# Attention block and MLP on one core: turned tiles loaded behind their stores, six residual tiles put into their PSUM bank, differences in another order, w2 jobs moved

## The chip, the cores and the metric

The kernel runs on one core of one Trainium2 chip. The metric is the device time of one execution in microseconds (us); lower is better. TensorE multiplies matrices, VectorE (DVE), ScalarE (ACT) and GpSimd (POOL) work on tiles of 128 partitions, and SyncE (SP) and GpSimd issue most DMA transfers. Each engine runs its instructions in the order in which they stand in the program; a wait on one holds up all behind it on that engine.

## The reference: what is computed

One transformer block on `x` (2048 tokens of 512 floats), all in float32, with a linear attention of 32 heads of 16 and an MLP of width 1792. Six rows of 512 (shifts, scales and gates) come from the condition `c`.

```python
mod = (silu(c) @ w_mod).reshape(1, 6, 1, -1)
sa, ca, ga, sb, cb, gb = (mod[:, i] for i in range(6))
h = layernorm(x) * (1 + ca) + sa
q, k, v = heads(h @ wqkv)
pq, pk = phi(q), phi(k)                 # t + 1 where t > 0, else exp(t); plus 1e-6
o = (pq @ (pk^T v)) / (pq . sum(pk) + 1e-6)
x = x + ga * (o @ wo)
h = layernorm(x) * (1 + cb) + sb
x = x + gb * (mish(h @ w1 + b1) @ w2)
```

## The kernel before, in words

**Numbers.** A float32 product is made of three: each operand is split into an upper part `..h` (ACT, L82) and a lower part `..l`, the rest (DVE, L88), and upper x upper, upper x lower and lower x upper are added up in one PSUM bank (`mm3`, L72). One such matmul of 128x512 is a row of 0.23 us on TensorE.

**Blocks and units.** The tokens are four blocks `b` of 512, each four tiles `t` of 128. A bank is a tile of tag `acc` (four buffers), `h` (three) or `tp` (one). After the attention's sums, these units follow on TensorE, named by what they write:

- `q_unit(b, g)` (L330): the queries of a block, 12 matmuls.
- `attend(b)` (L878): the denominators `den`; DVE makes `rden` of them, a DMA stores it (`rden_d`, L890), four DMAs read it back, each row for 16 partitions (`rd`, L894), and DVE multiplies the queries by it (L902), before they are split into `qs_g h` and `qs_g l` for the four groups `g`. For blocks 0 and 1 POOL issues these DMAs, for 2 and 3 SP.
- `o_unit(b, t)` (L921), here unit n = 4b + t: 12 matmuls of `qs` with the output matrix `m`. `o_post` (L912) adds the residual tile `r` (that is `x`) to the bank on DVE (L914).
- For blocks 0 and 1 `norm_first` (L928) follows: the sums of the row and of its squares on ACT (`act_sums`, L213; for tiles 2 and 3 of block 1 bn_stats on DVE), the power -1/2 on POOL (L199), the normalised tile `n` on ACT (L208), and `turn` (L235), a transpose of 32x32 squares on DVE into a buffer `wide` (L239), of which there is one. After a block's last tile `spread` (L241) stores `wide` in DRAM in four DMAs (L245), and `load_squares` (L249) loads the turned block in four (L252). `WAIT` says how many steps the loads stand behind the stores: three for block 0, one for block 1.
- `turned_f` (L983): ACT scales the loaded tile into `hf_n` (L256). The first MLP product works on blocks 0 and 1 at once, as a 2x2 block product in seven multiplications; `columns` (L990) makes the differences `t1` to `t4` of the four `hf_n` of a column half c on DVE (L995), and all are split: b11, b21, b22, t1 to t4.
- `pair_begin` (L1146) multiplies a11 with b11 for a pair g of MLP columns, and ACT copies it to a second bank `p11` (L1149). `pair_early`, `pair_middle` and `pair_end` (L1166 to L1190) make the other products, the next ones with b21, t2, t1 and t3. `d_unit` (L1111) is the second MLP product of one column tile `f`.
- `w2_job(f)` (L707) multiplies tile f of `w2` with the gate `gb` on DVE (L716), splits it and has POOL store both parts (L728); `w2_sums(g)` (L739) makes the differences of tiles 2g and 2g + 1 for the last two blocks, which are done with seven products too.

**What sets the order.** The program is written out by hand. Work beside TensorE is a generator that is started by `spawn`; every `tick()` runs each for one more step, so a `yield` puts the rest one tick later. `order` (L1074) says at which unit n the turned tiles are scaled on ACT: block 0 at n = 9 and 11, block 1 at 12 and 13. `load_w2(0)` and `(1)` come at n = 4, `(2)` and `(3)` at n = 7, where `w2_job(0)` and `w2_job(1)` start too. Two `pair_begin` follow n = 13, then n = 14 and 15, then the pairs.

## Time and profile before

| | us |
|---|---|
| median of 3 runs | 495.13 |
| lowest and highest | 493.16, 496.28 |
| the profiled execution, its own time | 495.35 |
| its span, first to last instruction | 493.6 |

TensorE is busy for 477.6 us of the span (97%), DVE for 396.8 (80%), ACT for 306.2 (62%), POOL for 119.6 (24%). The granted clock of TensorE was 0.993 of full speed in the mean.

How to read the views. A row of the timeline has the start of an instruction in us, its duration, the engine, the line, and out<-in; in brackets stands the idle time before it and what ended that. Instructions on an engine overlap a little, so the distance of two starts is what one costs in a row. Names in the profile leave buffer numbers out: `qs_0h` is the upper part of group 0, whichever block. SPq and POOLq are DMA issues. In the table by stretches the columns are the stretch, busy time of each engine with the count of instructions, the granted clock, the DMA engines' busy share and GB/s.

### The profile page before, as it was taken

The numbers are of one execution on the slowest core, as the hardware profiler recorded it, in microseconds if no ns is written. First come the engines' busy times: TensorE is split into PE (matmuls) and PEld (weight loads), VectorE is DVE, ScalarE is ACT, GpSimd is POOL, SyncE is SP. The second block draws the span as 40 slices with busy tenths as digits, with TensorE's granted clock in tenths as the row PEclk, the third lists the DMA queues.
The fourth block names the chain that finished last, engine by engine and source line by source line (L and its number), as shares of the span: only waits on it lengthen the run. The fifth ranks groups of instructions, "written<-read, shape, count | busy, mean of one in ns | idle before, by whom it ended". The sixth has DMA issues, their size and how long they took to land.

```text
span 493.6 us, 7008 instructions
## 1 busy us (share of the span) xinstructions
PE 477.6 (97%) x2290; PEld 388.7 (79%) x2290; DVE 396.8 (80%) x791; ACT 306.2 (62%) x549; POOL 119.6 (24%) x200
## 2 busy tenths in 40 slices
PE   8999999999999995889999999999999999999997
PEld 6688777768878883678888888888888888888887
DVE  6899897998999895898799874599535678769993
ACT  6787469756656863678777764696055677547600
POOL 3573121000023122113225323233111101263400
PEclk9999999999999998899999999999999999999999
DMA  8905759534874449856468827998472523486974
GB/s 295 378 10 93 185 112 275 190 129 123 255 203 106 139 119 283 265 175 212 160 203 277 233 87 189 390 323 225 122 200 64 107 46 79 113 212 146 233 154 109
DMA packets 86399, 89.10 MB, mean 180 GB/s; under 512 B 22961, under 2 KB 59321, under 8 KB 86362
## 3 DMA queue, kind: packets, MB, share of 16 engines
q1 hardware_dynamic: 61320, 53.37, 37.9%
q0 software_dynamic: 22784, 34.49, 26.1%
q10 hardware_dynamic: 2258, 0.79, 0.8%
q8 instruction: 18, 0.29, 0.2%
q14 instruction: 19, 0.16, 0.1%
HBM read 59.52 MB, written 27.00 MB: 175 GB/s over the span
## 4 chain that ended last, share of the span: by engine, by line
PE 66%; DVE 16%; DMA 9%; ACT 4%; SPq 2%; issue 1%; POOL 1%; DVEq 0%; ACTq 0%
PE p_a L1139 15%; PE p_s L1139 8%; PE oacc L76 5%; PE oacc L75 5%; PE oacc L74 5%; PE m L76 5%; PE m L74 5%; PE m L75 5%; PE p L1139 4%; DMA sq_x<-wide_x 3%; PE pq_a L376 2%; DMA w2r<-in_w_dram 2%; DMA sq_n<-wide_n 2%; DVE wm L175 2%; DVE q L290 1%; DVE q L902 1%
## 5 line engine op out<-in xcount | busy, mean ns | idle before, releaser
L1144 DVE TENSOR_TENSOR cb<-p_s,u 128x512 f32<-128x512 f32 x28 | 19.1, 685 | 11.3 <-ACT u L1179 11.3
L777 POOL DMA_DIRECT2D wb<-w2d x14 | 9.8, 705 | 67.3 <-issue 23.9
L1131 ACT ACTIVATE ub<-cb,b1c 128x512 f32<-128x512 f32 x28 | 20.0, 718 | 6.7 <-DVE cb L1144 6.5
L1149 ACT ACTIVATE p<-p_a 128x512 f32<-128x512 f32 x14 | 8.0, 578 | 24.2 <-PE p_a L1139 12.2
L199 POOL TENSOR_TENSOR rs_n<-rs_n,half 128x1 f32<-128x1 f32 x16 | 9.6, 602 | 52.0 <-DVE rs_n L225 43.3
L1430 POOL DMA_DIRECT2D wt_m<-w2t x20 | 14.0, 703 | 25.2 <-DVE cb L1144 12.4
L256 ACT ACTIVATE hf_n<-sq_n,mc 128x512 f32<-128x512 f32 x16 | 12.3, 807 | 10.8 <-DMA sq_n<-sq_n 10.8
L1179 ACT ACTIVATE u<-p_a 128x512 f32<-128x512 f32 x14 | 8.4, 598 | 17.0 <-PE p_a L1139 16.9
L1106 ACT ACTIVATE u<-p,b1c 128x512 f32<-128x512 f32 x14 | 9.6, 686 | 13.7 <-PE p L1139 13.7
L890 POOL DMA_DIRECT2D rden_d<-rden x2 | 1.5, 738 | 59.9 <-DVE rden L888 59.9
L1106 ACT ACTIVATE u<-p_a,b1c 128x512 f32<-128x512 f32 x14 | 9.6, 688 | 9.2 <-PE p_a L1139 9.1
L783 POOL DMA_DIRECT2D w2b<-w2d x20 | 10.6, 539 | 19.2 <-PE oacc L76 14.1
L74 PE MATMUL o<-m_0h,qs_0h 128*128 128x512 f32 x16 | 6.8, 428 | 6.4 <-ACT qs_0h L82 6.4
L290 DVE SCALAR_TENSOR_TENSOR ku<-e_k,relu_k 128x512 f32<-128x512 f32 x16 | 10.9, 682 | 2.0 <-ACT relu_k L288 2.0
L290 DVE SCALAR_TENSOR_TENSOR q<-e_q,relu_q 128x512 f32<-128x512 f32 x16 | 10.6, 685 | 1.4 <-ACT relu_q L288 1.4
L199 POOL TENSOR_TENSOR rs_x<-rs_x,half 128x1 f32<-128x1 f32 (+1 forms) x10 | 7.8, 787 | 15.9 <-DVE rs_x L194 15.1
L190 DVE BATCH_NORM_STATS2 st_x<-x 128x6 f32<-128x512 f32 x13 | 8.8, 676 | 3.2 <-DMA x<-in_x_dram 3.2
L919 POOL DMA_DIRECT2D x1d<-r x8 | 4.4, 548 | 28.3 <-DVE r L914 28.3
L287 ACT ACTIVATE e_k<-pk 128x512 f32<-128x512 f32 x16 | 9.4, 590 | 2.6 <-PE pk L76 1.7
L914 DVE TENSOR_TENSOR r<-o,r 128x512 f32<-128x512 f32 x16 | 10.8, 675 | 0.0
L175 DVE SCALAR_TENSOR_TENSOR wm<-wm,sc_row 128x512 f32<-128x512 f32 x16 | 10.5, 680 | 0.0
L299 POOL DMA_DIRECT2D ku<-ku x8 | 7.2, 940 | 13.5 <-DVE ku L290 13.5
(1661 smaller groups left out, 1880.9 us busy)
## 6 DMA issues: line engine op xcount, KB each, us to landing
wm<-in_wmodt_dram SPq DMA_DIRECT2D x24, 256.0 KB
w1p<-in_w_dram SPq DMA_DIRECT2D x24, 256.0 KB
w2b<-w2d POOLq DMA_DIRECT2D x20, 256.0 KB, 6.8
wt_m<-w2t POOLq DMA_DIRECT2D x20, 256.0 KB, 3.8
r<-in_x_dram SPq DMA_DIRECT2D x16, 256.0 KB
sq_n<-wide_n SPq DMA_DIRECT2D x16, 256.0 KB
sq_n<-sq_n SPq DMA_DIRECT2D x16, 256.0 KB
x<-in_x_dram SPq DMA_DIRECT2D x15, 256.0 KB
```

The costliest lines, as they stand in the source:

```text
L74: pe.matmul(o, st[0], mv[0], start=start, stop=False)
L75: pe.matmul(o, st[0], mv[1], start=False, stop=False)
L76: pe.matmul(o, st[1], mv[0], start=False, stop=stop)
L175: dve.scalar_tensor_tensor(t, t, 1.0, row, op0=ALU.mult, op1=ALU.mult, accum_out=mc[:, i:i + 1])
L199: pool.tensor_tensor(y, y, half[:, lo:hi], op=ALU.pow)
L256: act.activation(dst.rearrange("p (t a i) -> p t a i", t=4, a=4), turned.pop((key, b, j)).rearrange("p (a t i) -> p t a i", a=4, t=4), AF. ...
L290: dve.scalar_tensor_tensor(dst, e, 1.0, r, op0=ALU.min, op1=ALU.add)
L1106: act.activation(u, p, AF.Mish, bias=b1c[:, f:f + 1])
L1131: act.activation(u, p, AF.Mish, bias=b1c[:, f:f + 1])
L1139: pe.matmul(p, st, mv, start=onto is None and c == 0 and i == 0, stop=c == 1 and i == 2, skip_group_check=onto is not None)
L1144: dve.tensor_tensor(out, p, u, op=ALU.add)
L1430: pool.dma_start(v, w2t[g][:, :, SUM[name], :])
```

## The change

1. `WAIT` becomes (0, 0): a block's four turned loads stand right behind its four stores on SP. They so stand ahead of the `rden_d` store and the `rd` loads of block 3.
2. For six output tiles (block 0, and tiles 0 and 1 of block 1) ACT writes the residual into the bank ahead of the unit (`o_seed`), the 12 matmuls add to it, and ACT takes the bank to SBUF and sums its rows in one instruction. The squares' sum follows on ACT with other scale factors; DVE's addition falls away for these tiles.
3. `columns_early` takes the place of two calls of `columns(0, c)`: both column halves together, in the order t2, t1, t3, t4, b22, and b12 is no more split.
4. `load_w2(2)` and `(3)` come at n = 4. `w2_job(0)` and `(1)` leave n = 7 and go into the first pair stage, which has jobs 0, 1 and 2; stages 2 to 5 have two jobs, stage 6 jobs 11, 12 and 13. `w2_sums(0)` goes into the second `d_unit` phase (`W2_AT`).

```diff
--- before.py
+++ after.py
@@ -728,13 +728,13 @@
             pool.dma_start(w2d[g, i][:, n, :], w2s[f][i])
         if g in SUMS_KEPT:
             pool.dma_start(w2f[g][:, n, :], t)
-        elif g < KEPT and n:
+        elif g in (1, 2) and n:
             for _ in range(1 if g else 6):
                 yield
             yield from w2_sums(g)
 
     w2t, w2k, wb = {}, {}, {}
-    W2_AT = {0: 6, 2: 5}
+    W2_AT = {0: 6, 1: 0, 2: 5}
 
     def w2_sums(g):
 
@@ -909,9 +909,19 @@
 
     x1d = {}
 
-    def o_post(p, b, t):
+    def o_seed(b, t):
+        p = seeds[b, t] = ps("acc", f"o_{b}_{t}")
+        act.activation(p, xt["r", b, t], AF.Copy)
+
+    seeds, first_sums = {}, {}
+
+    def o_post(p, b, t, seeded):
         r = xt["r", b, t]
-        dve.tensor_tensor(r, p, r, op=ALU.add)
+        if seeded:
+            s_ = first_sums[b, t] = cst.tile([P, 2], F32, tag="osum", name=f"osum_{b}_{t}", bufs=6)
+            act.activation(r, p, AF.Identity, accum_out=s_[:, 0:1])
+        else:
+            dve.tensor_tensor(r, p, r, op=ALU.add)
         if b >= 2:
             yield
             if t == 0:
@@ -919,15 +929,38 @@
             pool.dma_start(x1d[b][t], r)
 
     def o_unit(b, t, tag="acc"):
-        p = ps(tag, f"o_{b}_{t}")
+        seeded = (b, t) in seeds
+        p = seeds.pop((b, t)) if seeded else ps(tag, f"o_{b}_{t}")
         ts = slice(P * t, P * (t + 1))
         for g in range(4):
-            mm3(p, [q[:, ts] for q in qs[b, g]], ms[g], g == 0, g == 3)
-        spawn(o_post(p, b, t))
+            st, mv_ = [q[:, ts] for q in qs[b, g]], ms[g]
+            for i, (l, r) in enumerate(((st[0], mv_[0]), (st[0], mv_[1]), (st[1], mv_[0]))):
+                pe.matmul(p, l, r, start=not seeded and g == 0 and i == 0, stop=g == 3 and i == 2,
+                          skip_group_check=seeded)
+        spawn(o_post(p, b, t, seeded))
+
+    def later_sums(b, t):
+
+        s_, v = first_sums.pop((b, t)), xt["r", b, t]
+        if ("n", b) not in rs:
+            for d, name in (rs, "rs"), (nb, "nb"):
+                d["n", b] = cst.tile([P, 4], F32, tag=name, name=f"{name}_n_{b}", bufs=NB)
+        act.activation(sb(f"scrap_n_{b}_{t}"), v, AF.Square, scale=-1.0 * D, bias=s_[:, 0:1], accum_out=s_[:, 1:2])
+        return s_
 
     def norm_first(b, t):
 
-        if b and t > 1:
+        if (b, t) in SEEDED:
+            if b:
+                yield
+            s_ = later_sums(b, t)
+            yield
+            dve.tensor_scalar(rs["n", b][:, t:t + 1], s_[:, 1:2], 1.0 / D ** 3, EPS, op0=ALU.mult, op1=ALU.add)
+            ln_rstd("n", b, t, t + 1)
+            yield
+            dve.scalar_tensor_tensor(nb["n", b][:, t:t + 1], s_[:, 0:1], -1.0 / D, rs["n", b][:, t:t + 1],
+                                     op0=ALU.mult, op1=ALU.mult)
+        elif b and t > 1:
             ln_stats("n", b, t, xt["r", b, t])
             ln_eps("n", b, t, t + 1)
             ln_rstd("n", b, t, t + 1)
@@ -953,7 +986,16 @@
             for j in (0, 2, 1, 3):
                 load_squares("n", b, j)
 
-    WAIT = (3, 1)
+    SEEDED = [(0, 0), (0, 1), (0, 2), (0, 3), (1, 0), (1, 1)]
+    SEEDS = [(0, 0), (0, 1), (0, 2), (0, 3), (), (), (1, 0), (1, 1)]
+
+    def seed_next():
+        if SEEDS:
+            i = SEEDS.pop(0)
+            if i:
+                o_seed(*i)
+
+    WAIT = (0, 0)
 
     def norm_tile(b, t):
 
@@ -1000,6 +1042,46 @@
             for h in halves[max(n - 2, 0):n] + halves[n:n + 2]:
                 next(h, None)
             yield
+
+    def columns_early(c0):
+
+        b11, b12, b21, b22 = [[hf.pop((b, c + h)) for c in range(2)] for h in (0, 2) for b in (c0, c0 + 1)]
+        t = [[sb(f"t_{c0}_{c}_{i}") for i in range(4)] for c in range(2)]
+        todo = {}
+
+        def diff(c, i):
+            u, v = ((b12[c], b11[c]), (b22[c], t[c][0]), (b22[c], b12[c]), (b21[c], t[c][1]))[i]
+            dve.tensor_tensor(t[c][i], u, v, op=ALU.subtract)
+
+        def upper(name, c, v):
+            todo[name, c] = split(f"{name}_{c0}_{c}", v, op_b, (name, c))
+            next(todo[name, c])
+
+        for c in range(2):
+            diff(c, 0)
+            diff(c, 1)
+            upper("t2", c, t[c][1])
+        for c in range(2):
+            upper("t1", c, t[c][0])
+        yield
+        for c in range(2):
+            run(todo["t2", c])
+            diff(c, 2)
+            upper("t3", c, t[c][2])
+        yield
+        for c in range(2):
+            run(todo["t1", c])
+            diff(c, 3)
+            upper("t4", c, t[c][3])
+        yield
+        for name in "t3", "t4":
+            for c in range(2):
+                run(todo[name, c])
+        for c in range(2):
+            upper("b22", c, b22[c])
+        yield
+        for c in range(2):
+            run(todo["b22", c])
 
     def kv_side():
 
@@ -1059,11 +1141,13 @@
                 spawn(split(f"m_{k}", m_ps, ms, k))
         tick()
     for g in range(4):
+        seed_next()
         q_unit(3, g)
         tick()
         if g == 1:
             spawn_idle(early_rows[1])
             for t in range(4):
+                seed_next()
                 o_unit(0, t)
                 spawn(norm_first(0, t))
                 if t == 1:
@@ -1077,25 +1161,21 @@
             n = 4 * b + t
             for i, j in order.get(n, ()):
                 turned_f(i, j)
-                if (i, j // 2) != (1, 0):
-                    spawn(split_b(i, j, f"b{j // 2 + 1}{i + 1}"))
+                if not i:
+                    spawn(split_b(i, j, f"b{j // 2 + 1}1"))
             if n == 14:
                 break
+            seed_next()
             o_unit(b, t)
-            if n in (12, 13):
-                spawn(columns(0, n - 12, ("b11", "b12", "b21", "b22")))
+            if n == 13:
+                spawn(columns_early(0))
             if b == 1:
                 spawn(norm_first(1, t))
             if n == 4:
-                load_w2(0)
-                load_w2(1)
+                for f in range(4):
+                    load_w2(f)
             if n == 5:
                 spawn(attend(3, 3, sp))
-            if n == 7:
-                spawn(w2_job(0))
-                spawn(w2_job(1))
-                load_w2(2)
-                load_w2(3)
             tick()
 
 
@@ -1285,8 +1365,9 @@
             ahead(1, f)
         return unit
 
+    JOBS = {1: (0, 1, 2), 2: (3, 4), 3: (5, 6), 4: (7, 8), 5: (9, 10), 6: (11, 12, 13)}
     for g in range(1, G):
-        for f in (2 * g, 2 * g + 1):
+        for f in JOBS[g]:
             spawn(w2_job(f))
         if g + 1 < G:
             for f in (2 * g + 2, 2 * g + 3):
```

## The prediction

> **What bounds the kernel now.** I read the page's busy shares first, then who waits for whom between 170 and 222 us, then the timelines of TensorE, ACT, DVE and SP there, the chain of waits, and the table by stretches.
>
> ```profile
> PE 477.6 (97%) x2290; PEld 388.7 (79%) x2290; DVE 396.8 (80%) x791; ACT 306.2 (62%) x549; POOL 119.6 (24%) x200
> ...
> ACT hf_n L256 <- DMA sq_n<-sq_n: 10.8, 5, 6.4
> ...
> PE o L74 <- ACT qs_0h L82: 6.4, 1, 6.4
> ```
>
> TensorE is busy nearly throughout, so a gain can only come out of its idle time, and the largest idle pieces stand in one place. The timeline of TensorE has them:
>
> ```profile
> 188.48 0.39 PE L74 MATMUL o<-m_0h,qs_0h 128*128 128x512 f32 x1
> ...
> 190.98 0.39 PE L76 MATMUL o<-m_3h,qs_3l 128*128 128x512 f32 x1
> 197.81 0.80 PE L74 MATMUL o<-m_0h,qs_0h 128*128 128x512 f32 x1 [6.44 <-ACT qs_0h L82]
> ...
> 201.06 0.60 PE L75 MATMUL o<-m_2l,qs_2h 128*128 128x512 f32 x1
> 202.74 0.50 PE L76 MATMUL o<-m_2h,qs_2l 128*128 128x512 f32 x1 [1.09 <-DVE qs_2l L88]
> 203.08 0.39 PE L74 MATMUL o<-m_3h,qs_3h 128*128 128x512 f32 x1
> ...
> 216.70 0.39 PE L1139 MATMUL p_a<-t_1h,s_0h 128*128 128x512 f32 x1
> 218.33 0.50 PE L1139 MATMUL p_a<-t_1l,s_0h 128*128 128x512 f32 x1 [1.24 <-DVE t_1l L88]
> 218.67 0.39 PE L1139 MATMUL p_a<-t_1h,s_0l 128*128 128x512 f32 x1
> ```
>
> Unit 11 runs from 188.48 in steps of 0.227 us (2.50 / 11). Unit 12 should start at 191.21 and starts at 197.81: 6.60 lost. Its next seven steps take 3.25 instead of 1.59: 1.66 lost. The two steps round `qs_2l` take 2.02 instead of 0.45: 1.57. The two round `t_1l` take 1.97: 1.52. Together **11.35 us**. The table by stretches shows that the 1.66 are the clock, which is halved 3 to 4 us after TensorE fell idle:
>
> ```profile
> 194.00:195.00 1.00, 0.00 (x0) 0.00 (x0) 0.00 (x0) 0.00 (x0) 0.00 (x0) 0.83 1.12 360
> 195.00:196.00 1.00, 0.00 (x0) 0.00 (x0) 0.00 (x0) 0.81 (x1) 0.00 (x0) 0.50 1.19 370
> ```
>
> Why ACT was late: its queue, and the chain of waits behind it.
>
> ```profile
> 195.13 0.81 ACT L256 ACTIVATE hf_n<-sq_n,mc 128x512 f32<-128x512 f32 x1 [6.43 <-DMA sq_n<-sq_n]
> ...
> 197.15 0.61 ACT L82 ACTIVATE qs_0h<-q 128x512 fp32r<-128x512 f32 x1
> ...
> 171.35 3.53 SPq L245 DMA_DIRECT2D sq_n<-wide_n  x4
> ...
> 185.48 2.28 SPq L252 DMA_DIRECT2D sq_n<-sq_n  x4
> ...
> 179.29 2.47 DMA rden_d<-rden
> 181.81 0.59 SPq L894
> ...
> 184.51 8.14 DMA w2r<-in_w_dram
> 192.67 2.78 SPq L245
> 195.50 8.06 DMA sq_n<-wide_n
> ```
>
> `qs_0h` of block 3 stands on ACT behind `hf_n`, which waits for block 0's turned tiles. Their stores went out at 171.35, their loads only at 185.48, behind `rden_d`, four `rd` and two `w2r`, into DMA engines that are full (share 1.12 and 1.19 in the two stretches above). A `w2r` took 8.14 us there and held back the last store of block 1's turned tiles until 195.50; that one took 8.06.
>
> **The change part by part.** First the loads. SP's order before:
>
> ```order
> L245 DMA sq_n_0_2099<-wide_n_0_1976 32x16x128 x4
> L890 DMA rden_d_3_2160<-rden_3_2157 4x32x128
> L894 DMA rd_3_0_2162<-rden_d_3_2160 128x1x512
> L894 DMA rd_3_1_2164<-rden_d_3_2160 128x1x512
> L894 DMA rd_3_2_2166<-rden_d_3_2160 128x1x512
> L894 DMA rd_3_3_2168<-rden_d_3_2160 128x1x512
> L705 DMA w2r_2_2190<-in_w2_dram 128x512
> L705 DMA w2r_3_2192<-in_w2_dram 128x512
> L252 DMA sq_n_0_0_2229<-sq_n_0_2099 128x512
> ```
>
> and now:
>
> ```order
> L705 DMA w2r_2_2076<-in_w2_dram 128x512
> L705 DMA w2r_3_2078<-in_w2_dram 128x512
> L245 DMA sq_n_0_2106<-wide_n_0_1977 32x16x128 x4
> L252 DMA sq_n_0_0_2111<-sq_n_0_2106 128x512
> L252 DMA sq_n_0_2_2113<-sq_n_0_2106 128x512
> L252 DMA sq_n_0_1_2115<-sq_n_0_2106 128x512
> L252 DMA sq_n_0_3_2117<-sq_n_0_2106 128x512
> L890 DMA rden_d_3_2172<-rden_3_2169 4x32x128
> L894 DMA rd_3_0_2174<-rden_d_3_2172 128x1x512
> ```
>
> The loads need the stores landed, so SP now stands still until then, and `rden_d` and `rd` of block 3 queue behind. The wait on ACT goes (block 0's tiles land some 8 us before ACT asks for them at n = 9); what is late next is `rd`. For store to load the same pair of DMAs on block 2 and 3 of x gives the bounds, for `rd` POOL's rows and the row of its use:
>
> ```profile
> 42.21 3.40 SPq L245 DMA_DIRECT2D sq_x<-wide_x  x4
> 52.63 3.09 SPq L252 DMA_DIRECT2D sq_x<-sq_x  x4
> ...
> 65.55 3.40 SPq L245 DMA_DIRECT2D sq_x<-wide_x  x4
> 72.82 2.08 SPq L252 DMA_DIRECT2D sq_x<-sq_x  x4
> ...
> 203.64 1.79 SPq L252 DMA_DIRECT2D sq_n<-sq_n  x4
> ...
> rd<-rden_d POOLq DMA_DIRECT2D x8, 256.0 KB, 4.9
> ...
> 187.90 1.25 DVE L902 SCALAR_TENSOR_TENSOR q<-q,rd 128x512 f32<-128x512 f32 x2
> ...
> 206.46 0.81 ACT L256 ACTIVATE hf_n<-sq_n,mc 128x512 f32<-128x512 f32 x1 [3.06 <-DMA sq_n<-sq_n]
> ...
> 209.57 1.52 ACT L256 ACTIVATE hf_n<-sq_n,mc 128x512 f32<-128x512 f32 x2 [0.57 <-DMA sq_n<-sq_n]
> ```
>
> Stores to loads took 72.82 - 65.55 = 7.27, and 10.42 the other time. I take 8.0, nearer the low one, though two more `w2r` (0.5 MB) now run ahead of them. Stores at 171.3 as before; loads at 179.3; their issue 2.1 to 181.4; `rden_d` 2.5 to 183.9; the second `rd` issued at 184.55 and landed after 4.9 at 189.45 (bounds 2.8, a turned load from 203.64 to 206.46, and 6.1, from 181.81 to the use at 187.90 without a wait). Before, `rd` was there by 187.90, so this step gives back part of the gain. On DVE stands behind it:
>
> ```order
> L902 SCALAR_TENSOR_TENSOR q_3_1_1838<-q_3_1_1838,rd_3_1_2176 128x512
> L239 STREAM_TRANSPOSE wide_n_1_2231<-n_1_3_2238 128x16x32
> L924 TENSOR_TENSOR r_2_1_1465<-o_2_1_2245,r_2_1_1465 128x512
> L88 TENSOR_TENSOR qs_3_0l_2261<-q_3_0_1796,qs_3_0h_2260 128x512
> L88 TENSOR_TENSOR qs_3_1l_2265<-q_3_1_1838,qs_3_1h_2264 128x512
> L902 SCALAR_TENSOR_TENSOR q_3_2_2009<-q_3_2_2009,rd_3_2_2178 128x512
> L902 SCALAR_TENSOR_TENSOR q_3_3_2041<-q_3_3_2041,rd_3_3_2180 128x512
> L88 TENSOR_TENSOR b11_0_0l_2271<-hf_n_0_0_2241,b11_0_0h_2270 128x512
> L88 TENSOR_TENSOR b21_0_2l_2274<-hf_n_0_2_2243,b21_0_2h_2273 128x512
> L924 TENSOR_TENSOR r_2_2_1495<-o_2_2_2277,r_2_2_1495 128x512
> L88 TENSOR_TENSOR qs_3_2l_2294<-q_3_2_2009,qs_3_2h_2293 128x512
> ```
>
> Before, it went
>
> ```order
> L902 SCALAR_TENSOR_TENSOR q_3_1_1834<-q_3_1_1834,rd_3_1_2164 128x512
> L239 STREAM_TRANSPOSE wide_n_1_2237<-n_1_3_2244 128x16x32
> L88 TENSOR_TENSOR w2_0l_2247<-w2g_0_2210,w2_0h_2246 128x512
> L88 TENSOR_TENSOR w2_1l_2250<-w2g_1_2213,w2_1h_2249 128x512
> L914 TENSOR_TENSOR r_2_1_1465<-o_2_1_2257,r_2_1_1465 128x512
> ```
>
> so two rows of `w2` are gone and the rest kept its order; the transpose of block 1's last tile still waits for `rd`. At 0.60 a row (187.90: 1.25 for two) the transpose ends at X = 189.45 + 1.2 = 190.65 and `qs_3_2l` 5.4 later, 196.05. TensorE, running through, wants it eight steps into unit 12, at 193.02: **3.0 us of new wait**.
>
> From X hangs block 1 too: stores and loads 7.3, the loads' issue to the last `hf_n` 7.0 (before 7.45, from 203.64 to the end of the row at 209.57, with `x1d` stores between), so H = 205.05. The order on DVE then was
>
> ```order
> L995 TENSOR_TENSOR t_0_1_1_2427<-hf_n_1_3_2398,t_0_1_0_2426 128x512
> L995 TENSOR_TENSOR t_0_1_2_2428<-hf_n_1_3_2398,hf_n_1_1_2396 128x512
> L995 TENSOR_TENSOR t_0_1_3_2429<-hf_n_0_3_2331,t_0_1_1_2427 128x512
> L88 TENSOR_TENSOR t1_0_0l_2417<-t_0_0_0_2388,t1_0_0h_2416 128x512
> L88 TENSOR_TENSOR t2_0_0l_2420<-t_0_0_1_2389,t2_0_0h_2419 128x512
> L88 TENSOR_TENSOR b22_1_3l_2423<-hf_n_1_3_2398,b22_1_3h_2422 128x512
> L88 TENSOR_TENSOR t3_0_0l_2455<-t_0_0_2_2390,t3_0_0h_2454 128x512
> L88 TENSOR_TENSOR t4_0_0l_2458<-t_0_0_3_2391,t4_0_0h_2457 128x512
> L88 TENSOR_TENSOR t1_0_1l_2463<-t_0_1_0_2426,t1_0_1h_2462 128x512
> L88 TENSOR_TENSOR t2_0_1l_2466<-t_0_1_1_2427,t2_0_1h_2465 128x512
> ```
>
> and is now
>
> ```order
> L1054 TENSOR_TENSOR t_0_1_1_2390<-hf_n_1_3_2367,t_0_1_0_2389 128x512
> L88 TENSOR_TENSOR t2_0_0l_2396<-t_0_0_1_2386,t2_0_0h_2395 128x512
> L1054 TENSOR_TENSOR t_0_0_2_2387<-hf_n_1_2_2346,hf_n_1_0_2344 128x512
> L88 TENSOR_TENSOR t2_0_1l_2401<-t_0_1_1_2390,t2_0_1h_2400 128x512
> L1054 TENSOR_TENSOR t_0_1_2_2391<-hf_n_1_3_2367,hf_n_1_1_2365 128x512
> ```
>
> The last lower part of t2 comes four rows (2.4 us) behind the last `hf_n`, not ten. On ACT stand t2 and t1 ahead of the copy to `p11`: one difference and four rows, H + 2.9. TensorE wants `p11` after units 12, 13, two first products, 14 and 15 (60 steps) at 204.83. 207.95 is 3.1 late, the same delay as the one above and not beside it: I take **3.1** for both.
>
> The seeding: ACT gets six copies of 0.5 more, DVE loses six additions.
>
> ```profile
> 153.38 0.39 PE L74 MATMUL o<-m_0h,qs_0h 128*128 128x512 f32 x1
> ...
> 151.74 0.57 ACT L287 ACTIVATE e_q<-pq 128x512 f32<-128x512 f32 x1
> ...
> 160.00:180.00 20.00, 20.00 (x116) 16.27 (x116) 18.63 (x41) 17.39 (x35) 2.22 (x4) 1.00 0.53 144
> ...
> L1149 ACT ACTIVATE p<-p_a 128x512 f32<-128x512 f32 x14 | 8.0, 578 | 24.2 <-PE p_a L1139 12.2
> ```
>
> DVE saves 6 x 0.6 = 3.6 us, but ACT's queue, busy for 17.39 of these 20 us, eats most of it; I leave the last turned tile where it was. A seed must be there when its unit starts. The tightest is the second: its unit starts at 153.38, and the seed stands on ACT just ahead of the row at 151.74, so it ends near 152.3, a microsecond early. I cost seeds at nothing (0.5 each if that cover goes, 3.0 for six). The moved `w2` jobs take 1 MB of stores out of the full stretch; on POOL these now follow block 3's `x1d` stores, and the first to read them back is the second `d_unit` phase, 100 us later. DVE has room where jobs 0 and 1 go, less where `w2_sums(0)` goes:
>
> ```profile
> 220.00:240.00 20.00, 20.00 (x89) 16.53 (x89) 17.64 (x40) 13.85 (x26) 4.80 (x9) 1.00 0.70 223
> ...
> 320.00:340.00 20.00, 20.00 (x90) 16.55 (x89) 19.86 (x37) 15.46 (x27) 6.71 (x12) 1.00 1.02 320
> ...
> 322.35 0.68 DVE L88 TENSOR_TENSOR a_0l<-ub,a_0h 128x512 fp32r<-128x512 f32 x1
> ...
> 329.08 0.39 PE L74 MATMUL oacc<-w2b,a_0h 128*128 128x512 f32 x1
> ```
>
> One job is 0.7 + 0.6 on DVE (two multiplications by 256 columns, one row by 512); stages 2 to 5 keep two each, stage 1 gets one more and loses `w2_sums(0)`. That one is four rows of 0.34 and two of 0.6, 2.6 us, into a stretch in which DVE has none to spare; but the lower part `a_0l` is made there 6.7 us ahead of its unit (322.35 to 329.08), so TensorE doesn't see it. Cost of both: nothing, and 2.6 if that lead should be used up.
>
> **The sum.** The profiled execution, 495.35 (span 493.6 and 1.75 around it): -11.35 + 3.1 = -8.25, so 487.1. It lies 0.2 above the median of 495.13: **486.9**.
>
> The Trainium skill, DMA: Bandwidth & Descriptors, Anatomy of one DMA, gives about 2.0 us and the bytes by 436 GB/s for a transfer. By that the four stores (1 MB) would land 4.4 us after issue, not 7.3 to 10.4, and nothing would be late: 483.8, an estimate by that page. The rows here are of the same transfers, so I go by them. TensorE: Matmul & The Clock Gate, Part 1, has the clock fall after a whole idle window of about 3.4 us. By that rule a gap of 3 us costs itself alone; the stretches above agree so far.
>
> **The rivals.**
> - **All covered**, 483.8 (495.13 - 11.35). Stores 7.27 and `rd` in 2.8: X = 187.85, both waits under 0.4. For it: DVE has 3.6 + 1.4 us less to do there. Against: `rd` are 1 MB behind 1 MB of loads. 0.17.
> - **`rd` later still, and the clock falls**: stores 10.42 and `rd` 6.1 put X at 194.25, the wait at 6.8 and the halved clock at 1.7 more: 492.3. For it: two `w2r` more ahead of the stores. Against: the `w2d` stores and the `w2r` of 184.51 are gone. 0.13, a third of it below 490.2.
> - **It does not do what it says**: DMA engines stay full, the turned tiles arrive as late as before, and only t2's 1.52 go: 493.6. Against: six transfers fewer lie between stores and loads. 0.05.
> - **Slower: DVE becomes the bound of the pair stages.** If the moved jobs make each `d_unit` wait for its `w2` lower part, one job's 1.3 us, two units a stage, six stages: 16, so 502.9. It decides where DVE's 17.6 of 20 us grow beyond 20; the change adds 1.3 at most. 0.05.
>
> **How the numbers follow.** The forecast (wait between 0.5 and 5 us) has 0.60. A measurement tells about 1% here: below 490.2 is faster. Faster 0.60 + 0.17 + 0.04 = 0.81, within 1% 0.09 + 0.05 = 0.14, slower 0.05. The range goes from all covered, less the scatter of the runs, 483.2, to 491.3, into the late case.
>
> **What would show it.** Right: no wait of ACT for `sq_n` at n = 9, `qs_0h` no longer ahead of TensorE, the clock at 1.00 from 190 to 206; a wait of TensorE for `qs_2l` or `p11` of about 3 us; block 1's loads issued near 198 and not 203.64. Wrong: `rd` landed by 187 or after 192, a wait of TensorE for a seed, or a new wait after 220.

## The result, and the profile after

The changed kernel takes 489.93 us (median of 4 runs, 487.89 to 490.54) against 495.56 us for the kernel before, timed beside it (median of 4): ratio 0.9888, 95% interval 0.9842 to 0.9933. Timed once more, beside other kernels, it took 490.12 against 494.34 (0.9918, 0.9901 to 0.9935). It is faster by about 1%, inside the predicted range, and 3 us slower than the predicted time.

The profiled execution took 490.54 (span 488.8), against 495.35. These are the units' first rows on TensorE and the first step of the second pair with `t_1h`, as anchors, of the kernel before:

```profile
168.21 0.39 PE L74 MATMUL o<-m_0h,qs_0h 128*128 128x512 f32 x1
...
222.32 0.39 PE L1139 MATMUL p_a<-t_1h,s_0h 128*128 128x512 f32 x1
...
490.02 0.28 PE L76 MATMUL m<-wt_m,l_m_4l 128*128 128x256 f32 x1
```

and of the changed kernel:

```profile
167.25 0.39 PE L938 MATMUL o<-m_0h,qs_0h 128*128 128x512 f32 x1
...
217.51 0.39 PE L1219 MATMUL p_a<-t_1h,s_0h 128*128 128x512 f32 x1
...
485.21 0.28 PE L76 MATMUL m<-wt_m,l_m_4l 128*128 128x256 f32 x1
```

From the second anchor to TensorE's last step both take 267.70 us, to the hundredth: the whole change lies ahead of 222 us. Ahead of the first anchor (unit 4) lies 0.96, and the kernels below start unit 4 anywhere from 166.64 to 167.57; two of them (`e2_loads_only` at 167.05, `e12_w2_only` at 167.40) run the program of before up to there, so that this part is mostly scatter. Between the anchors, which I call **the stretch**, it is 54.11 before and 50.26 after: 3.85 us. With no wait at all the stretch would be 54.11 - 11.35 = 42.76, so 7.5 us are still lost in it, where the prediction left 3.1.

Where they are lost, in TensorE's timeline of the changed kernel (in brackets the idle time and what ended it):

```profile
190.02 0.39 PE L938 MATMUL o<-m_3h,qs_3l 128*128 128x512 f32 x1
190.38 0.50 PE L938 MATMUL o<-m_0h,qs_0h 128*128 128x512 f32 x1
190.72 0.40 PE L938 MATMUL o<-m_0l,qs_0h 128*128 128x512 f32 x1
193.35 0.50 PE L938 MATMUL o<-m_0h,qs_0l 128*128 128x512 f32 x1 [2.24 <-DVE qs_0l L88]
...
195.21 0.79 PE L938 MATMUL o<-m_2h,qs_2h 128*128 128x512 f32 x1 [0.66 <-ACT qs_2h L82]
...
197.56 0.80 PE L938 MATMUL o<-m_2h,qs_2l 128*128 128x512 f32 x1 [1.13 <-DVE qs_2l L88]
...
205.96 0.39 PE L938 MATMUL o<-m_0h,qs_0h 128*128 128x512 f32 x1
```

Unit 12 no longer waits for `qs_0h` ahead of its first step. It waits inside, for 2.24 + 0.66 + 1.13 = 4.03 us, and the steps behind run at half speed. Behind 205.96 the timeline marks no wait of TensorE up to the end of the stretch: the one for `t_1l` is gone, and nothing waits for a seed. The stretches show the clock (third column from the end):

```profile
191.40:194.80 3.40, 1.20 (x4) 0.67 (x4) 3.40 (x7) 1.94 (x4) 0.55 (x1) 1.00 0.76 187
194.80:198.20 3.40, 1.86 (x4) 1.04 (x5) 3.40 (x7) 3.40 (x6) 0.54 (x1) 0.50 0.97 246
198.20:201.60 3.40, 3.40 (x10) 2.63 (x9) 2.31 (x4) 0.02 (x1) 1.08 (x2) 0.50 0.77 226
```

Why the lower parts are late: SP's queue, and DVE behind it.

```profile
169.23 4.17 SPq L245 DMA_DIRECT2D sq_n<-wide_n  x4
178.69 1.77 SPq L252 DMA_DIRECT2D sq_n<-sq_n  x4
180.51 0.58 SPq L890 DMA_DIRECT2D rden_d<-rden  x1
184.25 2.50 SPq L894 DMA_DIRECT2D rd<-rden_d  x4
192.15 3.34 SPq L245 DMA_DIRECT2D sq_n<-wide_n  x4
199.86 1.79 SPq L252 DMA_DIRECT2D sq_n<-sq_n  x4
```

```profile
175.66 0.95 DVE L888 RECIPROCAL rden<-rden 128x128 f32<-128x128 f32 x1
...
188.97 0.69 DVE L902 SCALAR_TENSOR_TENSOR q<-q,rd 128x512 f32<-128x512 f32 x1 [4.47 <-DMA rd<-rden_d]
190.81 0.69 DVE L902 SCALAR_TENSOR_TENSOR q<-q,rd 128x512 f32<-128x512 f32 x1 [1.15 <-DMA rd<-rden_d]
191.42 0.70 DVE L239 STREAM_TRANSPOSE wide_n<-n 128x512 f32<-128x512 f32 x1
...
196.82 0.68 DVE L88 TENSOR_TENSOR qs_2l<-q,qs_2h 128x512 fp32r<-128x512 f32 x1
```

The divisor `rden` is ready at 176.61. Its store `rden_d` goes out at 180.51, since SP stands at block 0's loads until their stores have landed (169.23 to 178.69). In the end of that wait the DMA engines are all but empty (second column from the end, the share of their time):

```profile
176.00:177.00 1.00, 1.00 (x6) 0.84 (x5) 0.76 (x2) 0.68 (x2) 0.00 (x0) 1.00 0.12 35
177.00:178.00 1.00, 1.00 (x6) 0.82 (x5) 0.97 (x2) 0.00 (x0) 0.00 (x0) 1.00 0.07 22
178.00:179.00 1.00, 1.00 (x6) 0.83 (x5) 0.93 (x4) 0.00 (x0) 0.25 (x1) 1.00 0.01 3
```

### The profile page after: what moved, and what is told of

It reads as the page before. It is cut to its first block, busy times and chain, and to the rows that moved or that the text cites. A ratio compares the mean times of both kernels' runs of the same rounds, so it can differ in the third digit from the quotient of the medians.

```text
span 488.8 us, 7005 instructions
## 1 busy us (share of the span) xinstructions
PE 478.2 (98%) x2290; PEld 389.5 (80%) x2290; DVE 394.0 (81%) x785; ACT 309.1 (63%) x555; POOL 120.3 (25%) x200
## 4 chain that ended last, share of the span: by engine, by line
PE 81%; DVE 9%; DMA 4%; ACT 3%; issue 1%; POOL 1%; SPq 0%; DVEq 0%; ACTq 0%
PE p_a L1219 16%; PE p_s L1219 8%; PE o L938 6%; PE oacc L75 5%; PE oacc L74 5%; PE oacc L76 5%; PE m L75 5%; PE m L76 5%; PE m L74 5%; PE p L1219 4%; PE pq_a L376 2%; PE pq L74 2%; DMA sq_x<-wide_x 1%; PE pq L75 1%; PE pq L76 1%; PE pk L76 1%
## 5 line engine op out<-in xcount | busy, mean ns | idle before, releaser
L902 DVE SCALAR_TENSOR_TENSOR q<-q,rd 128x512 f32<-128x512 f32 x16 | 10.5, 686 | 5.7 <-DMA rd<-rden_d 5.6
L256 ACT ACTIVATE hf_x<-sq_x,mc 128x512 f32<-128x512 f32 x8 | 6.4, 802 | 5.5 <-DMA sq_x<-sq_x 5.5
```

Source lines behind the costliest of these rows:

```text
L256: act.activation(dst.rearrange("p (t a i) -> p t a i", t=4, a=4), turned.pop((key, b, j)).rearrange("p (a t i) -> p t a i", a=4, t=4), AF. ...
```

## The experiments

The theory after this reading was that SP's queue sets the stretch: block 0's turned loads, put right behind their stores, hold back `rden_d` and `rd`. (`w2r` are the loads of `load_w2`, 256 KB each, issued by SP; `w2d` are the stores of the jobs' split parts, 256 KB each, issued by POOL.) The rivals were that bytes hold `rd` back wherever it is issued, and that other parts of the change carry the gain. Every kernel was timed beside the kernel before, on the same chip:

| kernel | median us | before | ratio | 95% | stretch |
|---|---|---|---|---|---|
| changed | 489.93 | 495.56 | 0.9888 | 0.9842 to 0.9933 | 50.26 |
| changed, again (`e11_changed_again`) | 490.12 | 494.34 | 0.9918 | 0.9901 to 0.9935 | 49.59 |
| before, loads alone (`e2_loads_only`) | 495.65 | 494.21 | 1.0034 | 1.002 to 1.0048 | 55.48 |
| before, w2 alone (`e12_w2_only`) | 490.49 | 494.34 | 0.992 | 0.9903 to 0.9936 | 48.50 |
| changed, loads back (`e3_all_but_loads`) | 487.5 | 494.21 | 0.9857 | 0.9839 to 0.9875 | 47.85 |
| changed, w2 back (`e6_w2_back`) | 492.95 | 494.72 | 0.9967 | 0.995 to 0.9984 | 50.36 |
| changed, old differences (`e7_old_columns`) | 490.12 | 494.72 | 0.9919 | 0.99 to 0.9937 | 49.37 |
| changed, no seeds (`e8_no_seeds`) | 491.16 | 494.72 | 0.9937 | 0.9918 to 0.9955 | 51.78 |
| changed, two `w2r` back (`e10_w2r_late`) | 488.63 | 494.34 | 0.9898 | 0.9877 to 0.9918 | 47.53 |
| changed, `rd` by POOL (`e1_rd_pool`) | 487.94 | 494.21 | 0.9876 | 0.986 to 0.9893 | 47.91 |
| changed, waits filled (`e4_filled`) | 491.34 | 494.21 | 0.9937 | 0.992 to 0.9955 | 49.67 |
| `rden_d` ahead of the loads (`e5_rden_first`) | 487.0 | 494.72 | 0.9846 | 0.9822 to 0.987 | 46.63 |
| the same, DVE in another order (`e9_order_on_dve`) | 485.31 | 494.34 | 0.9812 | 0.9793 to 0.9832 | 45.76 |

The stretch is that of the one profiled run. That run was the fastest of its kernel for `e1_rd_pool`, `e4_filled`, `e6_w2_back`, `e10_w2r_late` and `e12_w2_only` (487.69, 489.61, 490.03, 487.86, 488.90), so there the stretch reads low, and the slowest for the changed kernel, `e8_no_seeds` and `e9_order_on_dve` (490.54, 492.15, 486.24), so there it reads high; the ratio decides. The rest of the program takes 267.67 to 267.71 in every one of them.

**`rd` from another queue.**

```diff
-                spawn(attend(3, 3, sp))
+                spawn(attend(3, 3, pool))
```

> The changed kernel with rden_d and rd of block 3 issued from POOL's queue instead of SP's, nothing else. Theory (SP's queue): the divisor is ready on DVE at 176.6 us, but rden_d goes out at 180.51 only, because it stands behind block 0's turned loads, which wait for their stores until 178.69. From POOL it goes out near 177, rd some 3 us later, and the two multiplications that waited until 188.97 and 190.81 run by 186. TensorE's three waits in unit 12 (2.2, 0.7, 1.1) and the halved clock behind them go, 7.4 us in all; block 1's last difference may then be 1 to 2 late for the copy to p11. 484.5, between 483 and 486. Rival (bytes): rd is late because the DMA engines are still full of w2r, stores and turned loads; then an earlier issue only lands slower, the multiplications move by less than 1.5 us, and the time is 488 to 490.

Measured 487.94 and not 484.5: a ratio of 0.9876, better than the changed kernel's second measurement (0.9918, by 2 us) and hardly better than its first (0.9888). `rd` went out 3.75 us earlier (180.50 for 184.25), and the multiplications with it ran at 188.03, one behind the other and without a wait for `rd`: 0.9 earlier than in the changed kernel for the first and 2.2 for the second. What kept them from 186 stands on POOL and, ahead of them, on DVE:

```profile
176.93 0.76 POOL L890 DMA_DIRECT2D rden_d<-rden  x1 [0.91 <-DVE rden L888]
180.50 2.41 POOL L894 DMA_DIRECT2D rd<-rden_d  x4 [2.81 <-DMA rden_d<-rden]
182.90 1.10 POOL L199 TENSOR_TENSOR rs_n<-rs_n,half 128x1 f32<-128x1 f32 x2
```

```profile
183.53 0.16 DVE L203 SCALAR_TENSOR_TENSOR nb_n<-mv_n,rs_n 128x1 f32<-128x1 f32 x1 [3.88 <-POOL rs_n L199]
...
188.03 1.25 DVE L902 SCALAR_TENSOR_TENSOR q<-q,rd 128x512 f32<-128x512 f32 x2
```

POOL, too, stands at `rd` until `rden_d` has landed, and the power for the norm (`rs_n`) queues behind it; DVE stands 3.88 us for that. The queue was right and the size was not: part of the wait had moved to another engine's queue. The clock stayed at 1.00.

**The loads alone.**

```diff
-    WAIT = (3, 1)
+    WAIT = (0, 0)
```

> The kernel before with the turned loads of both blocks issued right behind their stores, and nothing else of the change. Theory (the loads' place carries the gain): ACT's wait for block 0's turned tiles goes with the 6.6 + 1.7 us behind it; the wait for rd takes its place, as large as in the changed kernel (4 to 5 us with the clock) or 1 us larger since the stores go out 2.1 later; the old order of the first columns' differences, ten rows of 0.6 behind block 1's last tile, costs 1.5 to 3 again. 491.5, between 489.5 and 493.5. Rival (the seeding and the moved w2 jobs carry it): no gain that can be told, 494.5 to 496.

Measured 495.65 against 494.21: slower by 0.3%, and the interval leaves out 1. My theory of the result missed: the move that stands first in the change's name has no gain of its own. TensorE's waits in that kernel:

```profile
194.03 0.80 PE L76 MATMUL o<-m_0h,qs_0l 128*128 128x512 f32 x1 [3.37 <-DVE qs_0l L88]
...
198.24 0.80 PE L76 MATMUL o<-m_2h,qs_2l 128*128 128x512 f32 x1 [1.06 <-DVE qs_2l L88]
...
211.73 0.50 PE L74 MATMUL o<-m_0h,qs_0h 128*128 128x512 f32 x1 [1.93 <-DVE r L914]
```

The 6.4 us ahead of unit 12 are gone and come back as 3.37 + 1.06 for the parts of `rd`, with the clock at 0.50 from 193 to 203, and as 1.93 for a bank whose addition (`r`) stands on DVE behind the differences of block 1's late tiles. And block 1's loads came hardly earlier (203.64 before):

```profile
191.62 4.69 SPq L245 DMA_DIRECT2D sq_n<-wide_n  x4
203.09 1.78 SPq L252 DMA_DIRECT2D sq_n<-sq_n  x4
```

11.5 us for stores to land among two `w2r` and the `w2d` stores.

**All but the loads.** The same line the other way round, in the changed kernel.

```diff
-    WAIT = (0, 0)
+    WAIT = (3, 1)
```

> The changed kernel with the turned loads back where they were (three and one steps behind their stores); seeds, order of the differences and w2 jobs as changed. On SP rden_d and rd of block 3 now stand between block 0's stores and loads again, but no w2r. Theory (SP's queue): rden_d goes out near 176.7 when the divisor is ready, rd near 179.7, the turned loads near 182.2, so both are there by 188; the waits in unit 12 nearly go, and the time is 485, between 483 and 488. Then the gain comes as much from the w2r and w2d transfers taken out of this stretch as from the place of the loads. Rival (the place of the loads carries the gain): ACT waits for block 0's turned tiles as before, and the time is above 491.

Measured 487.5 (0.9857, 0.9839 to 0.9875), clear of the changed kernel's 0.9901 to 0.9935 in its second measurement and at the good end of the wider 0.9842 to 0.9933 of the first. SP now goes

```profile
176.85 0.59 SPq L890 DMA_DIRECT2D rden_d<-rden  x1
179.37 2.55 SPq L894 DMA_DIRECT2D rd<-rden_d  x4
182.09 1.76 SPq L252 DMA_DIRECT2D sq_n<-sq_n  x4
```

with `rd` 4.9 us earlier than in the changed kernel, and TensorE waits 1.72 us ahead of unit 12, for `qs_0h` behind the turned tiles. Inside the unit it still waits 0.67 for `qs_2h` and 1.62 for `qs_2l`, where the expectation had the waits nearly gone; but the clock stayed at 1.00, though one stretch had as little work as this:

```profile
193.10:196.50 3.40, 1.11 (x5) 0.30 (x3) 3.40 (x7) 3.03 (x5) 0.36 (x1) 1.00 0.48 123
```

So with the rest of the change in place, moving the loads brings nothing and costs some 2 to 3 us (487.5 against 489.93 and 490.12).

**w2 alone, and all but w2.** The first is the kernel before with these lines of the change, the second the changed kernel without them:

```diff
-        elif g < KEPT and n:
+        elif g in (1, 2) and n:
...
-    W2_AT = {0: 6, 2: 5}
+    W2_AT = {0: 6, 1: 0, 2: 5}
...
-            if n == 7:
-                spawn(w2_job(0))
-                spawn(w2_job(1))
-                load_w2(2)
-                load_w2(3)
...
-        for f in (2 * g, 2 * g + 1):
+        for f in JOBS[g]:
```

> The kernel before with the w2 jobs, loads and sums moved as in the change, and nothing else of it. Theory (w2's transfers and rows held back block 0's turned tiles, not the place of the loads): with two w2r and eight w2d transfers out of the way the turned loads are there at about 190 instead of 195.13, the gap of TensorE ahead of unit 12 shrinks from 6.6 us to 1.5 to 3.5, the stretch from 54.1 to 49 to 51, 490 us, between 489 and 491.5. Rival (w2 matters only together with the seeds and the new order of the differences, since the stretch is bound by several chains): the gap shrinks but the lateness comes back at t_1l and at a bank, 493 to 495.

> The changed kernel with the w2 jobs, their loads and the sums back where they were. Theory (w2's transfers and rows carry most of the gain): with the loads' place changed alone the time did not fall, and with all but the loads it fell most, so something else of the change frees this stretch; if it is w2, the four rows on DVE between rd and qs_3, and the 1 MB of stores and 0.5 MB of loads come back there and the stretch from unit 4 to the second pair grows from 50.3 to 53 or more: 493 to 496. Rival (the order of the first columns' differences carries it): 489 to 491 as the changed kernel.

w2 alone gives 490.49 (0.992): the whole gain of the change, as its theory expects, and against the rival. Without it the rest of the change keeps 0.3% of gain (0.9967). In the kernel with w2 alone the order on SP is that of before but for two `w2r`:

```profile
178.60 0.59 SPq L890 DMA_DIRECT2D rden_d<-rden  x1
181.13 2.61 SPq L894 DMA_DIRECT2D rd<-rden_d  x4
183.92 1.77 SPq L252 DMA_DIRECT2D sq_n<-sq_n  x4
```

```profile
190.63 1.71 ACT L256 ACTIVATE hf_n<-sq_n,mc 128x512 f32<-128x512 f32 x2 [4.87 <-DMA sq_n<-sq_n]
```

The turned tiles were there 6.7 us after the loads' issue (183.92 to 190.63); before, it was 9.65 (185.48 to 195.13). How much of this is the two `w2r` ahead of the loads, how much the `w2d` stores (the trace of before has four there, not eight), and how much the rows that DVE no longer does there, no run separates in that kernel. In the changed kernel one does in part: with the two `w2r` alone put back (`e10_w2r_late`, below) it has 0.9898, with all of w2 back 0.9967, so that there the jobs, their stores and rows, carry it and not the place of the `w2r`.

**The other two parts.** In the changed kernel the differences go back to `columns`, or the two lists of seeds are empty.

```diff
-                if not i:
-                    spawn(split_b(i, j, f"b{j // 2 + 1}1"))
+                if (i, j // 2) != (1, 0):
+                    spawn(split_b(i, j, f"b{j // 2 + 1}{i + 1}"))
...
-            if n == 13:
-                spawn(columns_early(0))
+            if n in (12, 13):
+                spawn(columns(0, n - 12, ("b11", "b12", "b21", "b22")))
```

> The changed kernel with the first columns' differences in the old order (all four of a column, then the parts; the lower parts of b12 and b22 of block 1 early). Theory (w2 carries most): the stretch grows by 1 to 2.5 us for t1 and t2 and for a bank that waits for a late addition, 490.5 to 492.5. Rival (the columns carry most): with the loads' place changed alone 4.05 us were lost behind unit 13, none of it in the changed kernel, so the stretch grows by 4 to 54.3: 493.5 to 495.

```diff
-    SEEDED = [(0, 0), (0, 1), (0, 2), (0, 3), (1, 0), (1, 1)]
-    SEEDS = [(0, 0), (0, 1), (0, 2), (0, 3), (), (), (1, 0), (1, 1)]
+    SEEDED = []
+    SEEDS = []
```

> The changed kernel without the six seeded banks (the additions and sums of block 0 and half of block 1 as before). Theory (the seeds cost and bring nothing by themselves, beyond some rows less on DVE): the stores of block 0's turned tiles, which went out at 169.23 here and at 171.35 before, go out some 1 to 2 us later and everything behind them with it: the stretch 50.5 to 52, 490 to 492. Rival (the seeds carry the gain, by the earlier stores): 493 to 496.

The old order of the differences costs nothing that can be told (0.9919). Its wait for `t_1l` of 1.53 us and one of 0.66 for a bank are there, and unit 12 lost less in that run (5.82 from its start to unit 13, against 8.49 in the second run of the changed kernel), with stores to loads in 7.32 us and `rden_d` to `rd` in 3.72 (7.60 and 4.99 there), so the profile of this one run does not settle what the order is worth. Without seeds it is 0.9937: about 1 us, but the intervals overlap. Block 0's stores went out 3.52 us behind unit 4's start, as against 1.79 to 2.80 in the kernels with seeds, and `qs_0h` stood late ahead of unit 12 as well (1.21 us). Together the two parts are worth more where the loads stay in their place: w2 alone has 0.992 (0.9903 to 0.9936), and w2 with these two and without the loads' move 0.9857 (0.9839 to 0.9875). That is some 3 us, about what the loads' move then takes away; no run says which of the two parts it is.

**The clock.** Zeros are added to unit 12's bank while it waits.

```diff
...
+    FILL = {(0, 2): 9, (2, 0): 2, (2, 2): 4}
...
+                for _ in range(FILL.get((g, i), 0) if (b, t) == (3, 0) else 0):
+                    pe.matmul(p[0:16, :], zero, ms[0][0], start=False, stop=False)
```

> The changed kernel with 15 multiplications by a zero block (16 columns by 512) set into unit 12 where TensorE waits, adding zeros to its bank: nine ahead of the first step with qs_0l, two ahead of the first with qs_2h, four ahead of the first with qs_2l. They fill 3.4 us of the 4.0 us of waiting. Theory (the idle time halves the clock): the clock stays at 1.00 from 195 to 202, where it was 0.50, and unit 13 ends 2 to 3 us earlier at the same waits: 487.5, between 486.5 and 488.5. Rival (the slow steps come from something else, or a gap costs itself alone): the steps stay at 0.43 us or the fillers cost time of their own, 489.5 to 492.

```profile
190.00:200.00 10.00, 9.10 (x38) 5.14 (x37) 9.70 (x16) 5.37 (x9) 1.63 (x3) 1.00 0.86 210
```

```profile
209.73 0.50 PE L1224 MATMUL p<-b_2h,a_0h 128*128 128x512 f32 x1 [0.83 <-ACT p L1234]
```

The clock stayed at 1.00, and from unit 12's start to unit 14's TensorE took 13.38 us (189.92 to 203.30) instead of 15.58 (190.38 to 205.96): 2.2 of the 2 to 3 expected. The mean granted clock was 0.999 or 1.000 in all six runs (0.992 to 0.996 in the eight of the changed kernel), so the idle time is what halved it. The time did not follow: 491.34 (0.9937), which is in the rival's range and no better than the changed kernel. In the profiled run 0.83 went to a wait for `p11` right behind and 0.32 to another after it; the other five runs, slower than this one, left no rows, and what they lost besides stays open. It was not the clock.

**The `w2r` ahead of the stores.**

```diff
-                for f in range(4):
-                    load_w2(f)
+                load_w2(0)
+                load_w2(1)
...
+            if n == 7:
+                load_w2(2)
+                load_w2(3)
```

> The changed kernel with the last two of the four w2r loads (0.5 MB) back behind rd; the w2 jobs stay moved. Theory (the w2r loads ahead make the turned stores land late, one of the two reasons why my 8.0 us was too short): from the stores to the loads SP takes 7.3 to 7.8 us instead of 9.46, rd goes out 1.5 to 2 us earlier, the stretch is 48 to 49 instead of 50.3: 488.5. Rival (the time to land scatters from run to run by itself, from 7.3 to 9.7 over the runs so far): no change outside the scatter, 489.5 to 491.

Measured 488.63 (0.9898) with stores to loads in 7.24 us, as the theory has it, though the intervals overlap. Over the runs with the loads right behind the stores that step took 9.46, 9.67, 8.73, 7.32, 9.22 and 7.60 us with four `w2r` ahead (mean 8.67), and 7.46, 7.70 and 7.24 with two (mean 7.47). Two `w2r` more go with about 1.2 us on the mean, but the kernels differ in other parts too, and the scatter with four is as large as what I tried to predict: the theory is likely and not shown.

**The changed kernel again.**

> The changed kernel itself once more, beside the three others on one chip, since it has four runs from 487.9 to 490.5 so far and versions of it lie 2 to 3 us apart. Both theories of the result say 489 to 491; if the time from the stores to the loads on SP scatters between 7.3 and 9.7, this run's unit 12 loses 3 to 8 us accordingly.

490.12; stores to loads 7.60, and the store of the divisor to the issue of `rd` 4.99 us, so that `rd` came no earlier for it.

**One wait beside the other.** SP has `rden_d`, the four loads, the four `rd`.

```diff
         queue.dma_start(bass.AP(tensor=d.tensor, offset=d.offset, ap=[[P, 4], [512, 32], [1, P]]), rden)
+        if b == 3:
+            for j in (0, 2, 1, 3):
+                load_squares("n", 0, j)
...
-            for j in (0, 2, 1, 3):
+            for j in (0, 2, 1, 3) if b else ():
```

> The changed kernel with block 3's rden_d moved ahead of block 0's turned loads on SP's queue, so that SP has rden_d, the four loads, then the four rd. Theory (SP's queue, one behind the other): the wait for the stores and the wait for rden_d now run side by side; rden_d goes out near 177, the loads near 179 as in the changed kernel, rd near 181 instead of 184.25, and both the turned tiles and rd are there by 187. From the start of unit 4 to the second pair's first step with t_1h TensorE takes 44 to 46.5 us (changed kernel 50.3, loads back in their place 47.9, with no wait 42.75): 485.5, between 483.5 and 487. Rival (the loads must stay behind rd, since their bytes hold rd back): rd issued at 181 but landed after 188, the stretch 48 or more, 487.5 to 490.

```profile
176.92 0.58 SPq L890 DMA_DIRECT2D rden_d<-rden  x1
178.76 1.76 SPq L252 DMA_DIRECT2D sq_n<-sq_n  x4
180.57 2.44 SPq L897 DMA_DIRECT2D rd<-rden_d  x4
```

```profile
193.84 0.60 PE L941 MATMUL o<-m_2h,qs_2l 128*128 128x512 f32 x1 [1.61 <-DVE qs_2l L88]
```

Issue times as expected, and 487.0 (0.9846, upper end 0.987, below the lower end of the changed kernel's second measurement, 0.9901, though not of its first, 0.9842), and DVE used the first two `rd` at 185.53 and 187.10, before the rival's 188: SP's queue it was, and not the bytes. But leaving the loads in their place gives the same within the noise (0.9857). The 1.5 us to 485.5 are in the last row and in the clock, which still halved for one stretch of 3.4 us:

```profile
190.70:194.10 3.40, 1.69 (x7) 0.79 (x6) 3.40 (x7) 3.28 (x6) 0.54 (x1) 1.00 0.97 239
194.10:197.50 3.40, 3.40 (x9) 2.65 (x9) 2.69 (x5) 0.40 (x1) 0.95 (x2) 0.50 0.72 222
```

**DVE in another order.** On top of that the last transpose of block 1 goes ahead of the multiplications with `rd` (which become a generator of their own, started at n = 9), and the parts of the first two `hf_n` come one step later.

```diff
...
+            if n == 9:
+                spawn(scale_q(3, last.pop()))
...
-                    spawn(split_b(i, j, f"b{j // 2 + 1}1"))
+                    part = split_b(i, j, f"b{j // 2 + 1}1")
+                    spawn(later(part) if n == 9 else part)
```

> The kernel with rden_d ahead of the turned loads, with two moves more on DVE and ACT: the transpose of block 1's last tile goes ahead of the multiplications with rd, and the parts of the first two columns' tiles go one step later, behind qs_2 and qs_3. Theory (what is left in unit 12 is DVE's queue behind rd): the lower part of qs_2 comes 1.8 us earlier, so the wait of 1.6 us and the slow steps after it go; block 1's stores go out near 185.5 instead of 188.44, so that the copy to p11 is there when TensorE comes 3.9 us earlier. From unit 4 to the second pair 43 to 44.5 us (rden_d ahead alone 46.6): 484, between 482 and 485.5. Rival (the earlier stores of block 1, 1 MB, run against rd's 1 MB and make both late): rd 1.5 us later, the stretch 46 to 48 and 486 to 488.

```profile
192.73 0.50 PE L949 MATMUL o<-m_2h,qs_2h 128*128 128x512 f32 x1 [0.67 <-ACT qs_2h L82]
194.07 0.50 PE L949 MATMUL o<-m_2h,qs_2l 128*128 128x512 f32 x1 [0.61 <-DVE qs_2l L88]
...
206.38 0.50 PE L1237 MATMUL p<-b_2h,a_0h 128*128 128x512 f32 x1 [0.20 <-ACT p L1247]
```

485.31 (0.9812, 0.9793 to 0.9832), the fastest version, 1% faster than the changed kernel. Unit 12 has no wait above 0.7 and the clock stays at 1.00. The stretch, 45.76, missed the 43 to 44.5: DVE used `rd` at 187.75 after 2.44 us of waiting, 2.2 later than the 185.53 of the kernel above, with its issue only 0.7 later. That is what the rival said of block 1's earlier stores (185.34 for 188.44), though no run takes them apart; its time, 486 to 488, did not come.

## Why the prediction was right or wrong

The range and the direction held: less time between the same two places, and a new wait for the lower parts behind `rd`. That the time fell into the range is in part luck, since the account behind it credits the wrong part of the change and leaves out the clock. Point by point:

- **The removed idle, 11.35.** Two of the four pieces went: ahead of unit 12 TensorE has 0.13 instead of 6.60, and the wait round `t_1l` is gone. The other two, slow steps at a halved clock and a wait for `qs_2l` (1.13 for 1.09), are there again. The forecast took them out and put a new wait in their place, which the third point answers.
- **What removes it.** Here the prediction's sum hid an error. It gave the removal to the loads' place and cost the w2 jobs at nothing. Alone, the loads' place takes away the wait ahead of unit 12 and loses as much behind `rd` (1.0034), and the w2 part gives all of the gain (0.992); with the rest in place, the loads' move loses 2 to 3 us. The 1 MB of `w2d` stores and the two rows less on DVE were named in the prediction, and given no price.
- **The new wait, 3.1: the term that failed.** The stretch was to be 45.86 and was 50.26, 4.4 worse. Of this 1.1 is the wait (4.03 + 0.13 against 3.1), 2.6 the clock (TensorE was busy for 1.86 + 3.40 us of the two halved windows, and at full speed half of that would do) and 0.7 small pieces at the ends of the waits. The prediction's "a gap of 3 us costs itself alone" was wrong: no gap reached 2.3 us, and the clock was at 0.50 for 6.8 us. Nor did the wait stand ahead of `qs_2l` alone, where the forecast had it: 2.24 of it came six steps earlier, at `qs_0l`.
- **The chain to the wait.** Stores left at 169.23, 2.1 ahead of "where it was": 0.96 by the earlier start of unit 4, the rest (1.98 behind that start, before 3.14) by the seeds. Stores to loads took 9.46 for 8.0, `rden_d` to `rd` 3.74 for 2.5, and the second `rd`, issued 0.6 behind 184.25, was there at 190.81 after 5.9 for 4.9; the loads' issue took 1.82 for 2.1. Together the last transpose ended at 192.1 for 190.65. The 2.5 was the row of before, where SP had issued nothing for 4 us: behind four turned loads that step took 3.72 to 4.99 in the eight runs that have it so, and 2.52 and 2.53 in the two that have it ahead.
- **`p11` is the same delay and not beside it.** Right: H was 207.25 (for 205.05; the prediction's own terms, 190.65 + 7.3 + 7.0, add up to 204.95), and TensorE, late itself, did not wait. When unit 12 got faster, as with the filled waits or `rd` by POOL, a wait of 0.83 or 0.51 for `p11` came up there.
- **Seeds at nothing.** Right on TensorE, which never waits for one. Without them the stores left later and the time was 1 us longer, which is not clear of the noise.
- **w2_sums and the later jobs at nothing.** Right: 267.70 us behind the second anchor in both.
- **The sum.** -8.25 became -4.81 in the profiled execution: 4.4 lost in the stretch, 0.96 won ahead of it by scatter. The truth lies between the forecast and the rival "`rd` later still, and the clock falls": the last transpose was 1.45 late and not 3.6 (194.25), and the clock fell all the same. (Between stores and loads stood seven transfers before, not the six of the third rival: `rden_d`, four `rd`, two `w2r`.)
- **The signs.** ACT had no wait for `sq_n` at n = 9, `rd` was there at 190.81, between 187 and 192, block 1's loads went out at 199.86 (near 198, not 203.64), and no wait came for a seed or after 220. The clock at 1.00 from 190 to 206 did not come.

The Trainium skill, TensorE: Matmul & The Clock Gate, Part 1, has a free-running window of about 3.4 us and the clock at half after an idle one. The length agrees: the halved stretches here last 3.4 (`rden_d` ahead of the loads) and 6.8 us (the changed kernel). The condition does not, if idle means empty: the window ahead of the fall was busy for 1.69 of 3.40 us in the one and 1.20 in the other. The 4.4 us that the prediction worked out for the four stores came from a fit that the Trainium skill, DMA: Bandwidth & Descriptors, Anatomy of one DMA, gives for transfers issued by GpSimd. The stores here go out from SP, and 9.46 us passed from their issue to that of the loads that wait for them.

## What to carry to other kernels

A DMA that waits for data to land blocks its queue as a slow instruction blocks an engine; put what is ready and wanted (here the store of the divisor) ahead of the waiting load, and let both receipts run side by side. Here that gained 0.4 to 0.7% on the changed kernel, and no more than issuing the loads later, behind `rd`, did. When a change has several parts, price each one alone and each one left out: here the part that gave the change its name cost time, and a part costed at nothing made the gain. Do not price a gap on TensorE by its length alone: in these kernels gaps of 0.6 to 2.4 us cost a halved window of 3.4 us (up to 1.7 us, if TensorE is busy throughout) or two in some runs, and none in others. And look at what comes next before you fill such a gap: here the clock stayed up, and the kernel was no faster.

## What the runs showed of the hardware that was not expected

- A window of 3.40 us in which TensorE was busy for 1.69 (50%) was followed by one at half clock, with no single gap over 1.7 us in it. The same gap of 1.6 us with others round it (1.72, 0.67 and 1.62 with the loads back) left the clock at 1.00, even though a stretch of 3.40 us there had TensorE busy for 1.11 only. So the place of the gaps against a fixed window seems to decide; no run sets a threshold.
- Block 0's four stores, 1 MB in all, took 7.24 to 9.67 us from issue until the load that waits for them went out, in the nine runs that have that load right behind them; the changed kernel alone had 9.46 in one run and 7.60 in another, and in the first of these the DMA engines were all but empty for its last 2.7 us (share 0.12 to 0.01). What the load still waited for there, no run shows.
- A store of 64 KB was 2.52 us from its issue to that of the load that waits for it when no other transfer was issued on SP just ahead of it, and 3.72 to 4.99 right behind 1 MB of loads.
